# A fused attention and mixture-of-experts kernel: one mask cast moved from VectorE to ScalarE, and the first batch's local queries and keys loaded as runs of nine tokens

## The chip, the cores and the metric

The kernel runs on one core of a Trainium2 chip. The metric is the device time of one execution in microseconds (us), the median of several runs. TensorE (PE) multiplies matrices, VectorE (DVE) and ScalarE (ACT) work element by element and empty PSUM, GpSimd (POOL) does the rest; SyncE (SP) and ACT issue the DMAs that matter here.

## What is computed

Attention over 4 batches, 8 heads, 576 tokens and 64 numbers a head, then a mixture of 8 experts with one expert for each token, then a second MLP over all 2304 tokens. The first four heads see the 32 tokens up to their own (local), the last four see every 32nd token (strided).

```python
scores = scale * np.matmul(q, k.transpose(0, 1, 3, 2))          # (4, 8, 576, 576)
mask_local = (rel >= 0) & (rel < stride)                        # stride = 32
mask_strided = (rel >= 0) & (pos[None, :] % stride == pos[:, None] % stride)
masks = np.stack([mask_local if h < H // 2 else mask_strided for h in range(H)], axis=0)
attn = softmax(np.where(masks, scores, -1e9))
x = (attn @ v).transpose(0, 2, 1, 3).reshape(B * S, H * D)      # 2304 x 512
e_idx = np.argmax(x @ w_gate, axis=1)
out[mask] = gate_w * eom * (relu(x[mask] @ w1[e]) @ w2[e])      # for each expert e
h = np.maximum(out @ w_in, 0.0); result = (h * h) @ w_out
```

## The kernel before

**Stages.** The program runs through attention of batches 0 to 3, then gates and routing, the eight experts, the second MLP, and the stores. Instructions are recorded through a tile framework whose scheduler sets the order on every engine; DMAs that are marked `keep_in_program_order` keep theirs on SP's queue.

**Loads.** `load_s` (L271) brings queries (`qs`) and keys (`ks`) of the strided heads, `load_l` (L283) those of the local heads (`ql`, `kl`), `load_v` the values. For batch 0, `qs` and `ks` are started at L150 and L152 on two queues, and the masks `msk` at L153 on ACT's. A local load is four DMAs per tensor, one a head, each 64 partitions x 9 x 64: partition g gets the tokens g, 64+g, 128+g, ..., nine pieces of 256 bytes.

**Transposes.** `transposes` (L322) makes steps of three: three transposes of 128x128 (L337) into one PSUM tile of the tag `tp` (two buffers), then `evac`, which copies the tile to `qsT`, `ksT`, `qlT` or `klT`, by turns on DVE (L316, L318 where the queries are scaled) and ACT (L320). A `ks` step needs two such copies, for the zero-padded form that the strided scores want. For batch 0 the strided steps come first, the queries' three and then the keys' three, and after each a few products whose result nobody reads (`turn_over`, L229) keep PE occupied. In a local step a 128x128 block holds two heads: the even head in columns 0 to 63, the odd in 64 to 127, so that the transposed block has the even head on partitions 0 to 63 and the odd on 64 to 127.

**Scores.** Each score tile begins with a product of the identity in bf16 and a mask in bf16 (L413 strided, L369 local; both read `cstb`), and the scores are added onto it: L427 for the strided heads (18 columns of the array each, side by side in groups of 32), L382 for the local ones. `cstb` gets the identity at L158 and the two masks at L159, both casts on DVE. After the scores come maximum (L384, L438), exponent (L388, L441, ACT), normalising, transposes of the probabilities (L462, L469) and the products with the values (L486 and L501, 64 columns of the array each). `rw` (L555) is the product for gates.

**At the start of the program** POOL clears padded tiles (L245 to L296) while the first loads arrive.

Of the kernel before, what the change touches and what calls it, by code (L numbers as in the profile page):

```python
# [7 lines left out]
F32 = mybir.dt.float32  # L8
# [4 lines left out]
AF = mybir.ActivationFunctionType  # L13
# [6 lines left out]
B, H, S, HD = 4, 8, 576, 64  # L20
P = 128
# [69 lines left out]
C_ML = C_IO + CAPS[0] - C0  # L91
C_ML0 = C_ML + KW
C_MS = C_ML0 + KW
C_TRI = C_MS + SM
# [3 lines left out]
C_BF = C_ML - P  # L98
# [33 lines left out]
def moe_kernel(ctx, tc, q, k, v, wg, wog, w1, w2, w_in64, w_out64, consts, out, dbg=None):  # L132
    nc = tc.nc
# [5 lines left out]
    fro = front.enter_context(tc.tile_pool(name="att_front", bufs=1, side="right"))  # L139

    cst = const.tile([P, C_ML], F32, name="cst")
    msk = fro.tile([P, C_END - C_ML], F32, name="msk")
# [11 lines left out]
    ident = cst[:, C_ID : C_ID + P]  # L154
    onesb = big.tile([P, P], BF16, name="onesb")
    nc.vector.memset(onesb, 1.0)
    cstb = big.tile([P, C_END - C_BF], BF16, name="cstb")
    nc.vector.tensor_copy(cstb[:, :P], ident)  # L158
    nc.vector.tensor_copy(cstb[:, P : C_TRI - C_BF], msk[:, : C_TRI - C_ML])  # L159
    identb = cstb[:, :P]  # L160
    trib = cstb[:, C_TRI - C_BF : C_IA - C_BF]
    pmh = big.tile([P, LATE, P], BF16, name="pmh")
# [63 lines left out]
    def turn_over(to, n, ins=None):  # L226
        for _ in range(n):
            with tc.issue_after(ins.ins) if ins else nullcontext():
                ins = nc.tensor.matmul(to, onesb, onesb[:, None, :].to_broadcast([P, 4, P]), start=True, stop=True)  # L229
        return ins  # L230
# [21 lines left out]
    NS, NL_ = S * 4 // P, S * 2 // P  # L252
# [6 lines left out]
    for i in range(NPT):  # L259
        if i < 2:  # L260
            x = big.tile([P, 4, 4, NG, SM], F32, name=f"ptp{i}")
            nc.gpsimd.memset(x, 0.0)
            ptp.append(x)
        x = big.tile([P, 4, NG, 32], F32, name=f"prp{i}")
# [3 lines left out]
    def go(o, i, kept=True):  # L268
        ins = nc.sync.dma_start(o, i)
        return tc.keep_in_program_order(ins) if kept else ins  # L270
# [11 lines left out]

    def load_l(b, t):  # L283
        for nm, src in (("q", q), ("k", k)):
            t[nm + "l"] = x = fro.tile([P, NL_, 2, HD], F32, name=f"{nm}l{b}", tag=nm + "l", bufs=1)
            for h in (0, 2, 1, 3):
                to = x[h // 2 * HD : h // 2 * HD + HD, :, h % 2, :]
                go(to, src[b, h].rearrange("(n g) d -> g n d", n=NL_), b < 2)

    def load_v(b, t):  # L290
        t["vs"] = x = vsp[b % 3]
# [12 lines left out]
    def load(b):  # L304
        t = load_s(b)
        load_l(b, t)
        load_v(b, t)
        return t
# [3 lines left out]
    def evac(out_ap, in_ap, scale=None):  # L312
        cnt_ev[0] += 1
        if EVP[cnt_ev[0] % len(EVP)]:
            if scale is None:
                nc.vector.tensor_copy(out_ap, in_ap)  # L316
            else:
                nc.vector.tensor_scalar(out_ap, in_ap, scale, None, op0=ALU.mult)  # L318
        else:
            nc.scalar.activation(out_ap, in_ap, AF.Copy, scale=1.0 if scale is None else scale)  # L320

    def transposes(b, t):  # L322
        t.update(trs[b % 2])
        for kind in "sl":
            steps = [(n0, nm) for n0 in range(0, 9, 3) for nm in "qk"]
            if b == 0:
                steps.sort(key=lambda x: x[1] == "k")
            for n0, nm in steps:
                yield
                ps = pss.tile([P, 3, P], F32, name=f"t{kind}{b}{nm}{n0}", tag="tp")  # L330
                x = t[nm + kind]
                late1 = b == 1 and kind == "s" and n0 == 0
                for i in range(3):
                    n = n0 + i
                    src = x[:, 2 * HD * n : 2 * HD * (n + 1)] if kind == "s" else x[:, n].rearrange("p j d -> p (j d)")
                    with tc.issue_after(lead["pt"].ins) if late1 else nullcontext():
                        ins = nc.tensor.transpose(ps[:, i, :], src, ident)  # L337
                if b == 0 and kind == "s":
                    turn_over(idle, HEAD[1 if (n0, nm) == (6, "q") else 2], ins)
                    lead["ts"] = ins  # L340
                y = t[nm + kind + "T"]
                if kind == "l":
                    y = y.rearrange("d h (n g) -> d n h g", n=9)[:, n0 : n0 + 3]
                    evac(y, ps.rearrange("d n (h g) -> d n h g", h=2), 0.125 if nm == "q" else None)
                    continue
                z = ps.rearrange("d n (h g) -> d h g n", h=4)
                if nm + kind == "ks":
                    y = y.rearrange("d h u (a g n) -> d u a h g n", a=3, n=3)[:, :, n0 // 3]
                    for j in range(2):
                        r = slice(j * HD, (j + 1) * HD)  # L350
                        evac(y[r, j], z[r])
                    continue
                y = y.rearrange("d h (a g n) -> d a h g n", a=3, n=3)[:, n0 // 3]
                evac(y, z, 0.125 if nm == "q" else None)
# [155 lines left out]

    tiles = {0: load_s(0)}
    load_l(0, tiles[0])
    q2, q3 = [], []

# [250 lines left out]
    def route(b, ts, lg, rows):  # L765
# [69 lines left out]
        else:  # L835
            weigh()

    tg = transposes(0, tiles[0])
    for _ in range(2 * 3 + 1):
        next(tg)  # L840
    tiles[1] = load_s(1)
    load_v(0, tiles[0])
    load_l(1, tiles[1])
    tables()
    load_v(1, tiles[1])
    nc.gpsimd.memset(zero, 0.0)
    nc.sync.dma_start(x_d[0].rearrange("(p c) -> p c", c=P), zero)
    for b in range(B):
        t = tiles[b]
        tn = transposes(b + 1, tiles[b + 1]) if b + 1 < B else iter(())  # L850
        for n, ku in enumerate(ORDER[b].split()):
            kind, u = ku[0], int(ku[1:])
# [36 lines left out]
    r = lambda nm, sh, dt=F32: const.tile([P] + sh, dt, name=nm)  # L889
# [370 lines left out]
    def e_l1(k, f):  # L1260
        C = CAPS[k]
        c, i = f * P // UC, f % (UC // P)
        u = ("w1", k, c)
        if k == 0:
            ahead(u, 5, max(units.index(u) + 3 + f % 2, min(units.index(u) + 5, 2 * NF1 // 2)) - units.index(u))
        else:
            with tc.issue_after(lead["relu"].ins), tc.issue_after(lead["step"].ins):
                ahead(u, 5, 3 + f % 2, 7)
        wh, wl = get(("w1", k, c))
        xh, xl = xsp[k]  # L1270
        ps = psm.tile([P, 512], F32, name=f"h{k}_{f}", tag="h", bufs=2)
        for a in range(KD):
            s_ = slice(i * P, (i + 1) * P)
            mm3(ps[:, :C], wh[:, a, s_], wl[:, a, s_], xh[:, a, :C], xl[:, a, :C], a == 0, a == KD - 1)
        hh = raws.tile([P, CAPS[0]], F32R, name=f"hh{k}_{f}", tag="xr", bufs=HB)
        hl = raws.tile([P, CAPS[0]], F32R, name=f"hl{k}_{f}", tag="xr", bufs=HB)
        ia, iv = split_by[units[1 + f]] if k == 0 < f < 4 else (lead["xa"], lead["pm"])
        with tc.issue_after(ia.ins):
            lead["relu"] = nc.scalar.activation(hh[:, :C], ps[:, :C], AF.Relu)  # L1279
        with tc.issue_after(iv.ins):  # L1280
            lead["step"] = nc.vector.scalar_tensor_tensor(  # L1281
                out=hl[:, :C], in0=ps[:, :C], scalar=0.0, in1=hh[:, :C].bitcast(F32), op0=ALU.max, op1=ALU.subtract
            )
        return hh, hl
# [70 lines left out]
    for k in range(E):  # L1355
        for f in range(NF1):
            h = e_l1(k, f)
# [21 lines left out]
            if (k, f) in CONV:  # L1379
                n = CONV.index((k, f))  # L1380
# [335 lines left out]
```

## Time and profile before

| | |
|---|---|
| median of 3 runs | 779.6 us (778.9 to 780.54) |
| the profiled execution | 782.54 us |
| its span, first to last instruction | 780.7 us |
| mean granted TensorE clock | 0.994 of full speed |
| PE busy | 756.5 us, 97% of the span |
| PE's weight loads (PEld) | 678.4 us, 87% |
| DVE, ACT, POOL busy | 565.9, 460.4, 172.8 us |

The profile shows one execution, 2.9 us above the median of the runs. PE's share is high over the whole span, so what matters is where PE has gaps; the views by window and the timeline show those. A row of the timeline gives the start, the length, the engine, the line and operation, output and inputs, and the idle time of the engine before it with what ended it.

### The profile page before, as it was taken

Reading aid. Unit: us, or ns where it says so; the run is one execution under the profiler, and the core shown is the slowest. Engines: PE = TensorE matmul, PEld = TensorE weight load, DVE = VectorE, ACT = ScalarE, POOL = GpSimd, SP = SyncE. Lnnn points to the kernel's source line nnn. Section 1 sums busy time; section 2 is a strip of 40 time slices with the busy share of each in tenths; the row PEclk is TensorE's granted clock in tenths of the full one; section 3 lists DMA queues with packets and bytes.
Section 4 is the critical chain, followed back from the end, with each engine's and each line's share of the span. In section 5 each row is a group of like instructions: output and inputs, shape, how many; then the busy total and the mean of one; then the engine's idle time right before and its main releaser. Section 6 shows DMA issues by size and latency. Waiting matters only on the chain.

```text
span 780.7 us, 14501 instructions
## 1 busy us (share of the span) xinstructions
PE 756.5 (97%) x5429; PEld 678.4 (87%) x5429; DVE 565.9 (72%) x1074; ACT 460.4 (59%) x930; POOL 172.8 (22%) x168
## 2 busy tenths in 40 slices
PE   7999998999999999999999999999999999999995
PEld 4777777899998999999988889888988988989894
DVE  6868787873676888888798989896555687556442
ACT  2745645444553665657687767786555676566443
POOL 6100101036627555320031232122000003000002
PEclk9999999999999999999999999999999999999998
DMA  9999713684988999866454444444322234223002
GB/s 198 169 200 222 134 54 103 220 279 113 224 275 197 302 242 317 282 212 216 129 203 175 149 163 175 144 154 136 127 75 88 82 113 170 75 95 102 0 1 83
DMA packets 104114, 124.86 MB, mean 160 GB/s; under 512 B 39428, under 2 KB 76856, under 8 KB 104040
## 3 DMA queue, kind: packets, MB, share of 16 engines
q1 hardware_dynamic: 95736, 100.42, 45.5%
q0 software_dynamic: 7568, 22.70, 8.6%
q10 hardware_dynamic: 736, 0.76, 0.4%
q8 instruction: 44, 0.72, 0.4%
q14 instruction: 30, 0.25, 0.1%
HBM read 101.82 MB, written 22.04 MB: 159 GB/s over the span
## 4 chain that ended last, share of the span: by engine, by line
PE 56%; issue 30%; DVE 7%; DMA 2%; POOL 2%; ACT 1%; POOLq 0%; SPq 0%; ACTq 0%; DVEq 0%
PE y L1092 5%; PE y L1094 5%; PE y L1093 5%; PE h L1092 5%; PE h L1094 5%; PE h L1093 5%; PE o L1093 2%; PE o L1092 2%; PE o L1094 2%; PE rw L555 2%; POOL out_dram L1436 2%; PE wt L1171 1%; PE sc1l L382 1%; PE lr L732 1%; PE sc2l L382 1%
## 5 line engine op out<-in xcount | busy, mean ns | idle before, releaser
L1092 PE MATMUL o<-hwo,gh 128*128 128x512 f32 x288 | 113.7, 396 | 0.9 <-ACT gh L1406 0.7
L1093 PE MATMUL o<-lwo,gh 128*128 128x512 f32 x288 | 113.5, 395 | 0.0
L1403 ACT ACTIVATE rl<-rl 128x384 f32<-128x384 f32 x96 | 49.6, 517 | 85.7 <-DVE rl L1401 85.7
L1072 DVE TENSOR_TENSOR lw<-rw,hw 128x1024 fp32r<-128x1024 f32 x62 | 83.7, 1352 | 16.4 <-ACT hw L1068 14.6
L1094 PE MATMUL o<-hwo,gl 128*128 128x512 f32 x288 | 84.2, 395 | 0.4 <-DVE gl L1408 0.4
L1092 PE MATMUL h<-xh,hw 128*128 128x416 f32 (+7 forms) x256 | 80.4, 315 | 0.9 <-issue 0.7
L1408 DVE TENSOR_TENSOR gl<-rl,gh 128x384 fp32r<-128x384 f32 x96 | 55.8, 584 | 34.1 <-ACT rl L1407 33.6
L1094 PE MATMUL h<-xh,lw 128*128 128x416 f32 (+7 forms) x256 | 79.4, 310 | 0.4 <-issue 0.4
L1093 PE MATMUL h<-xl,hw 128*128 128x416 f32 (+7 forms) x256 | 79.3, 310 | 0.0
L1436 POOL DMA_INDIRECT out_dram<-ob,idx x18 | 23.1, 1284 | 252.5 <-ACT ob L1435 247.2
L1279 ACT ACTIVATE hh<-h 128x416 fp32r<-128x416 f32 (+7 forms) x64 | 28.2, 441 | 85.8 <-PE h L1094 69.1
L1093 PE MATMUL y<-hl,hw 128*128 128x416 f32 (+7 forms) x256 | 78.6, 310 | 0.0
L1094 PE MATMUL y<-hh,lw 128*128 128x416 f32 (+7 forms) x256 | 78.1, 310 | 0.3 <-issue 0.3
L1092 PE MATMUL y<-hh,hw 128*128 128x416 f32 (+7 forms) x256 | 74.3, 311 | 0.0
L1068 ACT ACTIVATE hw<-rw 128x1024 fp32r<-128x1024 f32 x62 | 65.2, 1055 | 4.4 <-issue 3.8
L1092 PEld LDWEIGHTS o<-hwo,gh 128*128 128x128 f32 x288 | 54.0, 188 | 11.7 <-ACT gh L1406 1.4
L1093 PEld LDWEIGHTS o<-lwo,gh 128*128 128x128 f32 x288 | 54.1, 188 | 10.0 <-DVE lwo L1072 0.5
L1094 PEld LDWEIGHTS o<-hwo,gl 128*128 128x128 f32 x288 | 53.4, 188 | 8.5 <-DVE gl L1408 0.9
L1281 DVE SCALAR_TENSOR_TENSOR hl<-h,hh 128x416 fp32r<-128x416 f32 (+7 forms) x64 | 31.2, 488 | 33.7 <-ACT hh L1279 28.7
L1407 ACT ACTIVATE rl<-rl 128x384 f32<-128x384 f32 x96 | 50.1, 522 | 2.3
L1406 ACT ACTIVATE gh<-rl 128x384 fp32r<-128x384 f32 x96 | 50.0, 521 | 1.9
L1092 PEld LDWEIGHTS h<-xh,hw 128*128 128x128 f32 x256 | 48.1, 188 | 1.2 <-DVE hl L1281 0.5
(626 smaller groups left out, 1926.3 us busy)
## 6 DMA issues: line engine op xcount, KB each, us to landing
rw<-in_moe_w_dram SPq DMA_DIRECT2D x62, 512.0 KB
rwa<-ws_d SPq DMA_DIRECT2D x24, 512.0 KB
rwb<-ws_d SPq DMA_DIRECT2D x24, 384.0 KB
e6wi<-in_moe_w_in_dram SPq DMA_DIRECT2D x32, 256.0 KB
rwo<-wout_d SPq DMA_DIRECT2D x16, 512.0 KB
x_d<-xr SPq DMA_DIRECT2D x18, 256.0 KB
ws_d<-eo POOLq DMA_DIRECT2D x16, 256.0 KB
s0wo<-in_moe_w_out_dram SPq DMA_DIRECT2D x8, 512.0 KB
```

The lines of the kernel that those rows point to most:

```text
L1068: ia = nc.scalar.activation(hi, raw, AF.Copy)
L1072: iv = eng.tensor_tensor(lo, raw, hi.bitcast(F32), op=ALU.subtract)
L1092: kept(nc.tensor.matmul(ps, ah, bh, start=first, stop=False))
L1093: kept(nc.tensor.matmul(ps, ah, bl_, start=False, stop=False))
L1094: lead["sum"] = kept(nc.tensor.matmul(ps, al, bh, start=False, stop=last))
L1279: lead["relu"] = nc.scalar.activation(hh[:, :C], ps[:, :C], AF.Relu)
L1281: lead["step"] = nc.vector.scalar_tensor_tensor(out=hl[:, :C], in0=ps[:, :C], scalar=0.0, in1=hh[:, :C].bitcast(F32), op0=ALU.max, op1=ALU ...
L1403: nc.scalar.activation(rl[:, :HC], src, AF.Relu)
L1406: nc.scalar.activation(hh[:, :HC], rl[:, :HC], AF.Square)
L1407: ia = nc.scalar.activation(rl[:, :HC], rl[:, :HC], AF.Square)
L1408: iv = nc.vector.tensor_tensor(hl[:, :HC], rl[:, :HC], hh[:, :HC].bitcast(F32), op=ALU.subtract)
L1436: ins = nc.gpsimd.indirect_dma_start(out=out[:, :], out_offset=bass.IndirectOffsetOnAxis(ap=idx[:, gt_, 0:1], axis=0), in_=ob, in_offset=None,
```

## The change

**The cast of the masks** leaves DVE. It becomes an ACT instruction that is recorded inside `transposes`, after the three transposes of the first `ks` step.

**The loads of batch 0's local heads** are cut another way. Partition g gets the tokens 9g to 9g+8, one run of 2304 bytes, and the tile is laid out by head, token, number instead of token, head, number. The other batches keep their loads.

**The transposes of these tiles** (batch 0, local) are cut in two. The even head's 64 columns are transposed into partitions 0 to 63 (L340 of the changed kernel), and the odd head's are multiplied with the identity in fp32 into partitions 64 to 127 (L341). So 18 transposes of 128 columns become 18 of 64 columns and 18 products. The copies out of PSUM write tokens 9g+n to their places, in as many instructions as before.

```diff
-    nc.vector.tensor_copy(cstb[:, P : C_TRI - C_BF], msk[:, : C_TRI - C_ML])
+    cstb_masks = lambda: nc.scalar.activation(cstb[:, P : C_TRI - C_BF], msk[:, : C_TRI - C_ML], AF.Copy)
...
     def load_l(b, t):
         for nm, src in (("q", q), ("k", k)):
-            t[nm + "l"] = x = fro.tile([P, NL_, 2, HD], F32, name=f"{nm}l{b}", tag=nm + "l", bufs=1)
+            sh = [P, NL_, 2, HD] if b else [P, 2, NL_, HD]
+            t[nm + "l"] = x = fro.tile(sh, F32, name=f"{nm}l{b}", tag=nm + "l", bufs=1)
             for h in (0, 2, 1, 3):
-                to = x[h // 2 * HD : h // 2 * HD + HD, :, h % 2, :]
-                go(to, src[b, h].rearrange("(n g) d -> g n d", n=NL_), b < 2)
+                r = slice(h // 2 * HD, h // 2 * HD + HD)
+                if b == 0:
+                    go(x[r, h % 2], src[b, h].rearrange("(g n) d -> g n d", n=NL_))
+                else:
+                    go(x[r, :, h % 2, :], src[b, h].rearrange("(n g) d -> g n d", n=NL_), b < 2)
...
                 for i in range(3):
                     n = n0 + i
+                    if kind == "l" and b == 0:
+                        nc.tensor.transpose(ps[:HD, i, :], x[:, 0, n, :], ident)
+                        nc.tensor.matmul(ps[HD:, i, :], x[:, 1, n, :], ident, start=True, stop=True)
+                        continue
...
+                if (b, kind, n0, nm) == (0, "s", 0, "k"):
+                    cstb_masks()
...
                 if kind == "l":
-                    y = y.rearrange("d h (n g) -> d n h g", n=9)[:, n0 : n0 + 3]
-                    evac(y, ps.rearrange("d n (h g) -> d n h g", h=2), 0.125 if nm == "q" else None)
+                    o = "d n h g" if b else "d h g n"
+                    if b:
+                        y = y.rearrange("d h (n g) -> d n h g", n=9)[:, n0 : n0 + 3]
+                    else:
+                        y = y.rearrange("d h (g n) -> d h g n", n=9)[:, :, :, n0 : n0 + 3]
+                    evac(y, ps.rearrange(f"d n (h g) -> {o}", h=2), 0.125 if nm == "q" else None)
                     continue
```

DVE's order at the start, before: the cast stands ahead of the copy of the third query step and of the first copies of the keys.

```order
L318 TENSOR_SCALAR qsT_128<-ts0q_166 128x4x96
L159 CAST cstb<-msk 128x210
L318 TENSOR_SCALAR qsT_128<-ts0q_178 128x4x96
L316 COPY ksT_130<-ts0k_188 64x4x96
L316 COPY ksT_130<-ts0k_195 64x4x96
```

The same piece of DVE's order after the change (lines of the changed kernel, whose numbers are a little higher); the cast is gone.

```order
L322 TENSOR_SCALAR qsT_127<-ts0q_165 128x4x96
L322 TENSOR_SCALAR qsT_127<-ts0q_177 128x4x96
L320 COPY ksT_129<-ts0k_187 64x4x96
L320 COPY ksT_129<-ts0k_195 64x4x96
```

ACT's order after the change: the cast stands between the copy of the second query step and ACT's first copy of the keys. Before, nothing stood there.

```order
L153 DMA msk<-in_consts_dram 128x210
L324 ACT_TABLE_LOAD
L324 ACTIVATE qsT_127<-ts0q_171 128x4x96
L159 ACTIVATE cstb<-msk 128x210
L324 ACTIVATE ksT_129<-ts0k_187 64x4x96
L324 ACTIVATE ksT_129<-ts0k_195 64x4x96
```

PE's order behind the first strided scores, before: `tl0q` and `tl0k` are the PSUM tiles of the local steps of batch 0, `sc0s` the two strided score tiles.

```order
L427 MATMUL sc0s_257<-ksT_130,qsT_128 18x2x18 x32
L337 MATMUL tl0q_302<-cst,ql_156 128x128 x3
L337 MATMUL tl0q_307<-cst,ql_156 128x128 x3
L427 MATMUL sc0s_317<-ksT_130,qsT_128 18x2x18 x27
L337 MATMUL tl0q_312<-cst,ql_156 128x128 x3
L427 MATMUL sc0s_317<-ksT_130,qsT_128 18x2x18 x5
```

The same place after the change, from the last pair of `tl0q_310` to the second score tile and the pairs of `tl0q_318`; the pairs of `tl0q_302`, ahead of them, and the nine of `tl0k` read the same way.

```order
L340 MATMUL tl0q_310<-cst,ql_155 64x128
L341 MATMUL tl0q_310<-cst,ql_155 64x128
L441 MATMUL sc0s_326<-ksT_129,qsT_127 18x2x18 x24
L340 MATMUL tl0q_318<-cst,ql_155 64x128
L341 MATMUL tl0q_318<-cst,ql_155 64x128
L340 MATMUL tl0q_318<-cst,ql_155 64x128
L341 MATMUL tl0q_318<-cst,ql_155 64x128
L340 MATMUL tl0q_318<-cst,ql_155 64x128
L341 MATMUL tl0q_318<-cst,ql_155 64x128
L441 MATMUL sc0s_326<-ksT_129,qsT_127 18x2x18 x8
```

Each transpose of 128 columns has become a transpose and a product by turns. The pairs stand where the steps of three stood, and the groups on PE are otherwise nearly in the same order: 24 and 8 of the second tile's scores instead of 27 and 5.

## Rows read from the trace of the kernel before

**Rows 1.** The page, busy time of an engine, its share of the span, instructions.

```profile
PE 756.5 (97%) x5429; PEld 678.4 (87%) x5429; DVE 565.9 (72%) x1074; ACT 460.4 (59%) x930; POOL 172.8 (22%) x168
```

**Rows 2.** Windows of 10 and 1 us: busy of PE, PEld, DVE, ACT, POOL; clock, DMA, GB/s.

```profile
0.00:10.00 10.00, 8.56 (x37) 3.98 (x37) 4.92 (x6) 2.26 (x3) 9.37 (x12) 1.00 0.94 195
10.00:20.00 10.00, 6.27 (x146) 4.60 (x147) 6.93 (x9) 1.92 (x5) 2.83 (x7) 0.83 1.03 200
20.00:30.00 10.00, 9.56 (x131) 7.39 (x128) 9.04 (x25) 7.73 (x33) 0.96 (x2) 1.00 1.01 182
...
10.00:11.00 1.00, 0.00 (x0) 0.00 (x0) 1.00 (x1) 0.00 (x0) 1.00 (x2) 1.00 1.38 180
...
15.00:16.00 1.00, 0.82 (x3) 0.15 (x1) 0.66 (x2) 0.43 (x1) 0.00 (x0) 0.50 0.81 184
```

**Rows 3.** Timeline of the head of the program, all engines.

```profile
4.68 3.56 POOL L250 MEMSET vsp<- 128x2048 f32 x2
...
6.82 0.56 DVE L318 TENSOR_SCALAR qsT<-ts0q 128x384 f32<-128x384 f32 x1 [2.12 <-PE ts0q L337]
...
8.92 4.04 DVE L159 CAST cstb<-msk 128x210 bf16<-128x210 f32 x1 [1.54 <-DMA msk<-in_consts_dram]
...
9.43 0.48 ACT L320 ACTIVATE ksT<-ts0k 64x384 f32<-64x384 f32 x1 [1.57 <-PE ts0k L337]
...
12.88 0.54 DVE L318 TENSOR_SCALAR qsT<-ts0q 128x384 f32<-128x384 f32 x1
...
13.47 0.55 PE L337 MATMUL ts0k<-cst,ks 128*128 128x128 f32 x3 [3.86 <-DVE qsT L318]
...
16.08 1.35 PE L427 MATMUL sc0s<-ksT,qsT 128*18 128x36 f32 x64 [0.26 <-DVE ksT L316]
```

**Rows 4.** The other cast of masks, L188, at 41.6 us (ns min/median/max).

```profile
L188 DVE CAST cstb<-msk x1: 303/303/303, 41.6 to 41.6; 128x292 bf16<-128x292 f32 x1
```

**Rows 5.** Timeline of PE: the local transposes of batch 0 and their neighbours.

```profile
17.36 0.96 PE L337 MATMUL tl0q<-cst,ql 128*128 128x128 f32 x6
...
18.25 1.20 PE L427 MATMUL sc0s<-ksT,qsT 128*18 128x36 f32 x54
...
20.39 0.82 PE L337 MATMUL tl0k<-cst,kl 128*128 128x128 f32 x6
...
21.54 0.55 PE L337 MATMUL tl0k<-cst,kl 128*128 128x128 f32 x3 [0.32 <-DVE klT L316]
...
22.01 0.78 PE L382 MATMUL sc0l<-klT,qlT 64*64 64x64 f32 x16
```

**Rows 6.** Operations of the tile tl0q: ns min/median/max.

```profile
L337 PE MATMUL tl0q<-cst,ql x9: 272/273/412, 17.4 to 19.7; 128*128 128x128 f32 x9
```

**Rows 7.** Timeline of PE: neighbours of one shape, then of different shapes.

```profile
24.90 0.66 PE L469 MATMUL pt0s<-cst,prp 128*128 128x128 f32 x4
25.39 0.49 PE L337 MATMUL ts1k<-cst,ks 128*128 128x128 f32 x3
...
45.73 0.76 PE L555 MATMUL rw<-igw,xT 128*128 128x144 f32 x4
...
48.86 0.30 PE L427 MATMUL sc1s<-ksT,qsT 128*18 128x36 f32 x2
49.10 0.64 PE L462 MATMUL pt1l<-cst,pr1l 128*96 128x128 f32 x4
49.67 0.30 PE L427 MATMUL sc1s<-ksT,qsT 128*18 128x36 f32 x2
49.90 0.55 PE L337 MATMUL ts2q<-cst,qs 128*128 128x128 f32 x3
```

**Rows 8.** Groups on PE from 40 to 60 us: busy us, mean ns.

```profile
L382 PE MATMUL sc1l<-klT,qlT 64*64 64x96 f32 x56 | 4.6, 254 | 0.0
L555 PE MATMUL rw<-igw,xT 128*128 128x144 f32 x20 | 3.8, 312 | 0.0
```

**Rows 9.** Timeline, SP's queue: the local queries of batch 0.

```profile
3.62 3.58 SPq L269 DMA_DIRECT2D ql<-in_q_dram  x4
```

## The prediction

> **What bounds the kernel now.** I read the page first: PE is busy for 756.5 of 780.7 us [rows 1]. What removes a gap of PE counts, what adds work to PE counts, and what other engines do counts where PE waits for it. The windows show where gaps are [rows 2]: PE is busy for 8.56 us of the first ten, 6.27 of the second and 9.56 of the third. So the second ten microseconds hold the one large hole: from 10 to 11 PE does nothing while DVE and POOL are busy all the time. After the hole the granted clock is at 0.50, the lower of its two levels (1.2 GHz), in the window from 15 to 16.
>
> The timeline names the hole [rows 3]. DVE starts the cast of the masks (L159) at 8.92, when `msk` has landed, and is in it for 4.04 us. Behind it on DVE stands the copy of the last query step, which runs only at 12.88. PE's second key step needs that copy's PSUM buffer and waits 3.86 us for it, until 13.47. The strided scores (L427) then begin at 16.08.
>
> Is it the cast that is slow, or all of DVE? A copy of 128x384 on DVE took 0.56 us at 6.82, in the middle of POOL's memsets, as long as the 0.54 at 12.88. The other cast of masks, 128x292 and thus wider, took 0.30 us at 41.6 [rows 4]. So it is that cast at that place, beside POOL, and the copies are not held with it.
>
> **Part 1, the cast to ACT: a gain at the head.** ACT is idle for 1.57 us until its first copy of the keys at 9.43 [rows 3], and the cast can start when `msk` has landed, 8.92. Its length on ACT for 210 columns is not shown; between the 0.30 us of DVE's 292 columns [rows 4] and the 0.48 us of that copy's 384 I take 0.40. It ends at 9.32, 0.11 before ACT is needed. It costs nothing, and a tenth or two if it is longer.
>
> On DVE the last query copy then no longer waits for 12.88. The key steps follow one another [rows 3]: ACT's copy at 9.43 shows that the first step is done by then, as it stays. The second, 0.55 us, comes behind one idle product, by my estimate at 9.6, so it ends at 10.15 and its copies (0.5 to 0.56) at 10.7. The third needs the buffer of the first, whose two copies, on both engines from 9.43, end at 10.0; so it starts at about 10.3, ends at 10.85, and its copies end at 11.4. The score masks run beside these copies. So L427 starts at 11.6 to 11.9 where it now starts at 16.08: 4.2 to 4.5 us. I allow 3.9 (PE or DVE steps a little worse placed) to 4.8 (the low clock after the hole goes too) and take **4.3 us less**.
>
> **Part 2, pairs in place of transposes: a cost on PE.** Before, the 18 transposes take two steps together and one alone for `tl0q` and the same for `tl0k`. From the start of a group to the start of the next these are 0.89 us (17.36 to 18.25), 0.82 (busy, 20.39) and 0.47 (21.54 to 22.01) [rows 5]; the single step of `tl0q` I count as the last. The sum is 0.89 + 0.47 + 0.82 + 0.47 = 2.65 us.
>
> After, 18 pairs stand there, each a transpose over 64 columns of the array and an fp32 product that fills the other 64. No row shows such a pair, so I bound it. A transpose takes 0.273 us [rows 6] and three of them 0.49 behind others of their shape [rows 7], so they follow each other at (0.49 - 0.273) / 2 = 0.11. The change of shape shows in the neighbours [rows 7]. `pt0s` lasts from 24.90 to 25.56, and `ts1k`, of its shape, starts at 25.39, 0.17 before that end. Between the narrow scores and whole-array transposes the next group starts only 0.06 to 0.07 before the end of the last: 49.16 against 49.10, 49.74 against 49.67, 49.97 against 49.90. So at each change of how the array is divided the pipeline empties almost wholly. The first transpose after it is also longer: three take 0.55 us instead of 0.49.
>
> If each half of a pair is such a change, a pair is:
> - the transpose, 0.27, or 0.33 if the 0.06 that three take longer falls to the first, less the overlap of 0.07: 0.20 to 0.26;
> - the product's two passes (a plain fp32 product shows as two instructions: `sc0s` stands 32 times in the order and 64 in the trace). The first lasts to the start of the second, no less than the 0.11 of a transpose and no more than the (0.76 - 0.31) / 3 = 0.15 of `rw`, four of which last 0.76 us [rows 7] at a mean of 0.31 [rows 8];
> - the second pass, between 0.25 (`sc1l`, 96 columns) and 0.31 (`rw`, 144), less 0.07: 0.18 to 0.24 [rows 8].
>
> That is 0.49 to 0.65 us; I take the middle, 0.57. Eighteen are 8.8 to 11.7, I take 10.2, and less 2.65 this is 6.2 to 9.0, taken **7.5 us more**. It lies on the path: from 20 to 30 us PE has only 0.44 us of gaps [rows 2], of which I let it fill 0.25. The maxima and exponents of batch 0 move back with it, and DVE and ACT have nothing else that could begin earlier instead. The gates, the experts and all that follows wait for attention, and PE is full there [rows 1], so a shift at 28 us arrives at the end.
>
> The Trainium skill, "TensorEngine Tiling (Array Packing)", Key Properties, says that changing the tiling mode drains TensorE. The overlap that falls from 0.17 to 0.07 us agrees with it; by that rule the change is at +3.0, without it at the -0.3 of the second rival below. The same page, Restrictions and Gotchas, says that column tiling excludes transposing fp32 on trn2; no row here shows it, and by it no transpose could run beside a product and the first rival below could not come.
>
> **Part 3, the loads: nothing.** SP issues the four query loads from 3.62 in 3.58 us [rows 9]. Until PE wants `ql`, now at about 12.9, 8 strided and 4 local loads of 144 KB, `msk` and `ident` must have landed, 1.9 MB; at 195 GB/s in the first ten us [rows 2] that is done at 10. The keys, 0.6 MB more at 200 GB/s, are there at 13 and wanted after 17. Runs of 2304 instead of 256 bytes only bring this forward. If their covers were gone they would show as a wait of PE for `ql`; the trace has none at 17.36 [rows 5]. The copies out of PSUM write rows in another order, as the strided steps' copies do now, at the 0.56 and 0.48 us in the rows of the head [rows 3].
>
> **The sum**, against the profiled execution of 782.54 us: -4.3 + 7.5 - 0.25 = +3.0, so 785.5. That execution is 2.9 above the median of the three runs, 779.6; the same difference on the median gives **782.6 us**. Its own range, both ends of both terms not met at once, is +1.4 to +4.8: 781.0 to 784.4.
>
> **The rivals.**
> - *The halves of a pair run side by side*, in two halves of the array, the transpose beside the product. Then a pair is two passes of 0.13, 18 x 0.26 = 4.7, +2.0 net, and the change is -2.3: 777.3, faster. For it: the narrow scores, which lie side by side in the array, follow each other at 1.35 / 64 = 0.02 us [rows 3]. Against: those are all products; a transpose beside a product is nowhere in the trace. It decides if a pair costs less than (2.65 + 4.3) / 18 = 0.39 us. Chance 0.16.
> - *One behind the other without emptying.* Then a pair is 0.11 + 2 x 0.13 = 0.37, 18 are 6.7, +4.0, and the sum -0.3: 779.3, no change that can be told. Against it is the overlap of 0.07 at every change of shape above. Chance 0.12.
> - *The cast is as slow on ACT.* If not DVE beside POOL but the place in time (the loads that arrive, DMA share 1.38 in the window from 10 to 11 [rows 2]) makes it 4 us, ACT's copy of the keys is held as DVE's was, nothing is gained, and it is +7.3: 786.9. Against: ACT's copy at 9.43 took 0.48 in that same time [rows 3]. Chance 0.04.
>
> **The numbers.** A measurement of this kernel can tell about 0.2%, 1.56 us, from no change. The forecast has 0.62, of which about 0.08 lies within 0.2%; the side-by-side case has 0.16, a third of it within 0.2%; the one-behind-the-other case, 0.12, is nearly all within; the slow cast, 0.04, is slower; 0.06 is for what I don't see, most of it faster. Faster 0.11 + 0.04 = 0.15, same 0.08 + 0.05 + 0.11 = 0.24, slower the other 0.61. The range takes the forecast's own and the first two rivals down to 777.0: 777.0 to 784.4. As the cases have both signs, the forecast's own 781.0 to 784.4 is the one to hold it to.
>
> **What would show it.** Right: the wait of 3.86 us is gone, L159 is an ACT row of about 0.4 us, L427 starts between 11.6 and 11.9 at the full clock (2.4 GHz), the 18 transposes and 36 passes of `tl0q` and `tl0k` take some 10 us from group to group, and the first local scores, at 22.01 now, start at about 25. Wrong: pairs that start under 0.39 us apart, an ACT copy of the keys later than 9.6, PE waiting for `ql` or `kl`, or a clock at 0.50 in a stretch where it is now full.

## The result: slower by 5 us, by more than forecast

The changed kernel takes 785.33 us in the median of 4 runs (784.86 to 786.14), the kernel before 779.98 (778.9 to 780.54): a ratio of 1.0068, with an interval of 1.0055 to 1.008, or +5.35 us. The way was forecast, the size was not: +3.0, with a range that ended at 784.4.

The page of the changed kernel has PE busy 8.4 us longer than before [rows 1] in a span that is 3.6 us longer.

```profile
span 784.3 us, 14572 instructions
...
PE 764.9 (98%) x5465; PEld 682.5 (87%) x5465; DVE 559.2 (71%) x1073; ACT 460.2 (59%) x931; POOL 172.4 (22%) x168
```

In windows of 10 us of the changed kernel (the columns of [rows 2]) the hole is gone. PE is busy for 8.89 us of the second ten instead of 6.27 [rows 2], the clock is granted in full there, and from 20 us on PE is full, with fewer instructions in it: 93 in the third ten instead of 131.

```profile
10.00:20.00 10.00, 8.89 (x150) 5.57 (x147) 3.70 (x8) 2.64 (x6) 2.82 (x7) 1.00 0.86 222
20.00:30.00 10.00, 9.83 (x93) 5.84 (x93) 3.99 (x11) 2.64 (x6) 0.67 (x1) 1.00 0.96 158
```

The timeline of the changed kernel shows the parts. The strided queries are transposed from 7.68 on, the cast is on ScalarE and takes 0.38 us, the strided scores (L441) start at 13.66 instead of 16.08 [rows 3], and the pairs follow each other at 15.52 - 14.92 = 0.60 and 16.11 - 15.52 = 0.59 us. The first local scores start at 28.56 instead of 22.01 [rows 5], and batch 1's local queries (`tl1q`) at 38.73.

```profile
7.68 0.49 PE L345 MATMUL ts0q<-cst,qs 128*128 128x128 f32 x3
...
9.95 0.38 ACT L159 ACTIVATE cstb<-msk 128x210 bf16<-128x210 f32 x1 [0.71 <-DMA msk<-in_consts_dram]
...
13.66 1.33 PE L441 MATMUL sc0s<-ksT,qsT 128*18 128x36 f32 x64 [0.70 <-DVE ksT L320]
...
14.92 0.30 PE L340 MATMUL tl0q<-cst,ql 128*64 128x128 f32 x1
...
15.15 0.43 PE L341 MATMUL tl0q<-cst,ql 128*64 128x128 f32 x2
...
15.52 0.30 PE L340 MATMUL tl0q<-cst,ql 128*64 128x128 f32 x1
...
16.11 0.30 PE L340 MATMUL tl0q<-cst,ql 128*64 128x128 f32 x1
...
28.56 1.44 PE L396 MATMUL sc0l<-klT,qlT 64*64 64x64 f32 x32 [0.17 <-DVE klT L320]
...
38.73 0.55 PE L345 MATMUL tl1q<-cst,ql 128*128 128x128 f32 x3
```

The delay settles early: `tl1q` starts 5.73 us later than in this execution of the kernel before (33.00, shown below), and the first expert's products (`h`) 5.37 us later. The first of these in the kernel before:

```profile
148.62 0.46 PE L1092 MATMUL h<-xh,hw 128*128 128x416 f32 x1
```

and in the changed kernel:

```profile
153.99 0.46 PE L1106 MATMUL h<-xh,hw 128*128 128x416 f32 x1
```

That the span differs by 3.6 only comes for the most part from the execution of the kernel before that was profiled first. It lost 0.31 + 1.09 = 1.40 us of PE time later on, from 235 to 265 us, which the same stretch of the changed kernel, 5 us later, did not. These are windows of 15 us, with columns as before, of the kernel before:

```profile
235.00:250.00 15.00, 14.69 (x99) 14.51 (x98) 10.53 (x17) 6.85 (x11) 9.89 (x10) 1.00 0.87 216
250.00:265.00 15.00, 13.91 (x90) 13.36 (x89) 10.46 (x18) 9.81 (x18) 9.37 (x12) 1.00 0.93 238
```

and of the changed kernel:

```profile
240.00:255.00 15.00, 15.00 (x102) 14.97 (x101) 11.86 (x19) 8.25 (x13) 9.85 (x11) 1.00 0.88 222
255.00:270.00 15.00, 15.00 (x101) 15.00 (x100) 8.92 (x16) 8.99 (x16) 8.58 (x11) 1.00 0.91 218
```

### The profile page after: what moved, and what is told of

Same layout as the page of the kernel before. It is cut to its first block, busy times and chain, and to the rows that moved or that the text cites. A ratio compares the mean times of both kernels' runs of the same rounds, so it can differ in the third digit from the quotient of the medians.

```text
span 784.3 us, 14572 instructions
## 1 busy us (share of the span) xinstructions
PE 764.9 (98%) x5465; PEld 682.5 (87%) x5465; DVE 559.2 (71%) x1073; ACT 460.2 (59%) x931; POOL 172.4 (22%) x168
## 4 chain that ended last, share of the span: by engine, by line
PE 58%; issue 30%; DVE 7%; POOL 2%; DMA 1%; ACT 1%; POOLq 0%; SPq 0%; DVEq 0%
PE y L1106 5%; PE h L1106 5%; PE y L1108 5%; PE y L1107 5%; PE h L1108 5%; PE h L1107 5%; PE o L1107 2%; PE o L1106 2%; PE o L1108 2%; PE rw L569 2%; POOL out_dram L1450 2%; PE idle L229 1%; PE wt L1185 1%; DVE xl L1325 1%; PE sc1l L396 1%
## 5 line engine op out<-in xcount | busy, mean ns | idle before, releaser
L1086 DVE TENSOR_TENSOR lw<-rw,hw 128x1024 fp32r<-128x1024 f32 x62 | 82.1, 1327 | 16.6 <-ACT hw L1082 16.5
```

Of the source, the lines that this page charges most:

```text
L1086: iv = eng.tensor_tensor(lo, raw, hi.bitcast(F32), op=ALU.subtract)
```

## The experiments

Ratios below are to runs of the kernel before on the same chip, whose medians were 781.2 us (`cast_only`, `pairs_pieces`, `grouped`, `two_products`), 780.53 (`cast_vl_late`, `runs_pairs_dve`, `dve_max`, `after_again`) and 781.34 (`half_runs`).

### The cast alone, and the old loads with the rest

`cast_only` has the cast on ScalarE and nothing else of the change.

```diff
-    nc.vector.tensor_copy(cstb[:, P : C_TRI - C_BF], msk[:, : C_TRI - C_ML])
+    cstb_masks = lambda: nc.scalar.activation(cstb[:, P : C_TRI - C_BF], msk[:, : C_TRI - C_ML], AF.Copy)
...
+                if (b, kind, n0, nm) == (0, "s", 0, "k"):
+                    cstb_masks()
```

> The kernel before with only the cast of the masks on ScalarE; loads and transposes as before. My theory: the hole of PE behind the cast goes and nothing is added, so the first strided scores start between 11.7 and 13.7 us instead of 16.08, and the time is 2.4 to 4.4 us under the kernel before (775.6 to 777.6). Rival 1 (the late first transposes of the changed kernel, 7.68 instead of 6.27, come from the new loads, which take DMA time from the strided queries): here they start at 6.3 and the scores at about 12.2. Rival 2 (they come from the clock of TensorE, which rose at 7.0 instead of 3.97 in that execution and made the 17 idle products longer): the start follows the time at which the idle products get short, whatever the loads are. Rival 3 (the gain is given back later in attention): the scores start early and the time is that of the kernel before.

Measured: 781.56 us, ratio 0.9993 (0.9982 to 1.0005). Rival 3 has it. In its profile the scores start at 12.48 instead of 16.08, and PE stays 3.75 us ahead of the kernel before until 29 us. Then it stands still for 2.95 us, for the local queries of batch 1, and the clock is granted at 0.66 over the ten microseconds that hold most of this wait. The products behind it are longer: 16 of `o0s` take 1.23 us here, and 0.72 in the kernel before (33.86, shown below). So the first expert's products come at 149.95, 1.33 us later than in the first profile of the kernel before, though `tl1q` came 0.63 us earlier. The timeline of PE in this run:

```profile
12.48 1.30 PE L429 MATMUL sc0s<-ksT,qsT 128*18 128x36 f32 x64 [0.71 <-DVE ksT L316]
...
29.12 0.30 PE L415 MATMUL sc1s<-cstb 128*128 128x288 bf16 x1
32.37 0.87 PE L337 MATMUL tl1q<-cst,ql 128*128 128x128 f32 x3 [2.95 <-DMA ql<-in_q_dram]
...
34.02 1.23 PE L503 MATMUL o0s<-ptp,vsp 128*64 128x72 f32 x16
```

and its windows:

```profile
20.00:30.00 10.00, 9.30 (x130) 7.28 (x126) 9.27 (x26) 9.81 (x44) 1.65 (x2) 1.00 1.02 182
30.00:40.00 10.00, 7.63 (x103) 6.25 (x103) 2.86 (x8) 2.73 (x8) 0.51 (x1) 0.66 0.93 166
```

`pairs_pieces` has all of the change but the nine-token runs.

```diff
-                r = slice(h // 2 * HD, h // 2 * HD + HD)
-                if b == 0:
-                    go(x[r, h % 2], src[b, h].rearrange("(g n) d -> g n d", n=NL_))
-                else:
-                    go(x[r, :, h % 2, :], src[b, h].rearrange("(n g) d -> g n d", n=NL_), b < 2)
+                to = x[h // 2 * HD : h // 2 * HD + HD, :, h % 2, :]
+                go(to, src[b, h].rearrange("(n g) d -> g n d", n=NL_), b < 2)
...
-                        nc.tensor.transpose(ps[:HD, i, :], x[:, 0, n, :], ident)
-                        nc.tensor.matmul(ps[HD:, i, :], x[:, 1, n, :], ident, start=True, stop=True)
+                        nc.tensor.transpose(ps[:HD, i, :], x[:, n, 0, :], ident)
+                        nc.tensor.matmul(ps[HD:, i, :], x[:, n, 1, :], ident, start=True, stop=True)
...
```

> The changed kernel with the old loads of 256-byte pieces: pairs and the cast on ScalarE stay, only the nine-token runs go. My theory: the loads are hidden, so the time is that of the changed kernel within 0.7 us (784.6 to 786.0), and a pair takes 0.59 us as there. Rival 1 (the runs delay the strided queries): 1.4 us under the changed kernel, 783.9, and the first transposes start at 6.3. A third view (the pieces are too slow for the earlier start of the local transposes): PE waits for ql or kl and the time is above the changed kernel.

Measured: 787.64 us, ratio 1.0064 (1.0048 to 1.008), the changed kernel's 1.0068 within the interval. (In us it is above the 786.0 expected, but on this chip the kernel before is 1.2 us slower too.) So beside the pairs the runs are worth nothing that can be told, and they do not delay the start either: the first transposes begin at 6.73 here, at 6.04 in a second profile of the changed kernel and at 7.68 in the first.

### What a pair costs

`grouped` puts the three transposes of a step first and its three products behind them.

```diff
                     if kind == "l" and b == 0:
                         nc.tensor.transpose(ps[:HD, i, :], x[:, 0, n, :], ident)
-                        nc.tensor.matmul(ps[HD:, i, :], x[:, 1, n, :], ident, start=True, stop=True)
                         continue
...
+                if kind == "l" and b == 0:
+                    for i in range(3):
+                        nc.tensor.matmul(ps[HD:, i, :], x[:, 1, n0 + i, :], ident, start=True, stop=True)
```

> The changed kernel with the three transposes of a step first and its three products after them, so that a step divides the array anew twice instead of six times. My theory (each change of the division waits until the instruction before is done): a step takes 0.165 + 0.109 + 0.23 + 0.16 + 4 x 0.107 + 0.203 = 1.30 us instead of 1.78, six steps 2.9 us less, 782.4. Rival (the product itself costs what the pair costs more, the change of division nothing): 1.78 us a step and 785.3.

Measured: 783.6 us, ratio 1.0025 (1.0012 to 1.0038), 0.0043 under the changed kernel's, which is 3.4 us (2.7 against the 1.0059 of the changed kernel's second set of runs, below). The same 9 passes of a step now take 15.37 - 14.12 = 1.25 us, where three pairs took 1.78. PE's timeline of this run, two groups of one step and the start of the next:

```profile
14.12 0.52 PE L340 MATMUL tl0q<-cst,ql 128*64 128x128 f32 x3
14.57 0.87 PE L347 MATMUL tl0q<-cst,ql 128*64 128x128 f32 x6
15.37 0.52 PE L340 MATMUL tl0q<-cst,ql 128*64 128x128 f32 x3
```

`two_products` makes the even head a product as well.

```diff
-                        nc.tensor.transpose(ps[:HD, i, :], x[:, 0, n, :], ident)
+                        nc.tensor.matmul(ps[:HD, i, :], x[:, 0, n, :], ident, start=True, stop=True)
```

> The changed kernel with a product by the identity in place of each 64-column transpose too, so that both halves are products, in two halves of the array, and nothing in a step divides the array anew. It has 72 passes where the changed kernel has 54 instructions. My theory: passes in the two halves run beside one another, a pass every 0.055 to 0.11 us, so a step of 12 takes 0.9 to 1.5 us instead of 1.78 and the time is 780.0 to 783.7. Rival (the passes of the products are what costs, not the change of division): 18 more passes of 0.11 to 0.16 us, 2 to 3 us above the changed kernel, 787.3 to 788.3.

Measured: 781.39 us, ratio 0.9996 (0.9983 to 1.001): 5.6 us under the changed kernel (4.9 against 1.0059), with 18 passes more. The two halves start 0.01 us apart, and six pairs of products take 15.44 - 13.98 = 1.46 us, 0.24 each with the exit, against 0.59. So a good part of a pair's price was the dividing anew: with two changes a step a pair is 1.25 / 3 = 0.42 us. The 0.24 has two causes, which this run does not separate: nothing inside a step divides anew, and the two halves run side by side. An estimate separates them. The six product passes of a step of `grouped` follow each other at (0.87 - 0.27) / 5 = 0.12 us, so three passes without a change would take 0.36; of the 0.59, then, 0.23 is the two changes, and what is below 0.36 comes from running side by side. PE's timeline of this run, the first four passes, the last, and what follows:

```profile
13.98 0.32 PE L340 MATMUL tl0q<-cst,ql 128*64 128x128 f32 x1
13.99 0.32 PE L341 MATMUL tl0q<-cst,ql 128*64 128x128 f32 x1
14.14 0.27 PE L340 MATMUL tl0q<-cst,ql 128*64 128x128 f32 x1
14.15 0.27 PE L341 MATMUL tl0q<-cst,ql 128*64 128x128 f32 x1
...
15.24 0.27 PE L341 MATMUL tl0q<-cst,ql 128*64 128x128 f32 x1
15.44 0.77 PE L441 MATMUL sc0s<-ksT,qsT 128*18 128x36 f32 x26
```

### What bounds the head

`cast_vl_late` is the cast alone with the local values of batch 0 loaded later.

```diff
-    load_v(0, tiles[0])
+    load_v(0, tiles[0], "s")
     load_l(1, tiles[1])
+    load_v(0, tiles[0], "l")
...
```

> The kernel with only the cast on ScalarE, and the local values of batch 0 loaded behind the local queries and keys of batch 1 instead of ahead of them. In the run of the cast alone PE was 3.75 us early until 29 us and then waited 2.95 us for the local queries of batch 1, in a stretch in which the DMA engines were busy all the time. Theory (the gain of the head is given back to the loads of batch 1): with these loads ahead of the values that wait goes, the gain stays, and the time is 2 to 4 us under the kernel before. Rival (the DMA engines as a whole are late, not one load): PE waits for the values at the first products with them (o0l, 35.1 us in the kernel before) instead, and the time is again that of the kernel before.

Measured: 781.13 us, ratio 1.0008 (0.999 to 1.0026). The rival has it: `tl1q` starts at 29.27 without a wait, and then the products with the values wait four times for `vl`, and the clock falls as well. But the profile is of the longest of twelve executions: 785.08 us, at a mean granted clock of 0.991. The shortest took 778.89 at 0.998, and no profile shows how long it waited. So that these waits give the whole gain back is shown for one execution and, for the others, only by the median. The waits of PE in this run from 20 to 60 us (in total, times, longest):

```profile
PE o0l L491 <- DMA vl<-in_v_dram: 2.3, 4, 0.8
```

and its windows:

```profile
30.00:40.00 10.00, 7.58 (x93) 5.42 (x92) 2.80 (x7) 2.65 (x7) 0.51 (x1) 0.77 0.95 174
40.00:50.00 10.00, 10.00 (x137) 7.16 (x137) 5.25 (x17) 3.89 (x14) 0.00 (x0) 0.72 1.10 203
```

`runs_pairs_dve` is the changed kernel with the cast back on VectorE, and `dve_max` the kernel before with the cast written as a maximum.

```diff
-    cstb_masks = lambda: nc.scalar.activation(cstb[:, P : C_TRI - C_BF], msk[:, : C_TRI - C_ML], AF.Copy)
+    nc.vector.tensor_copy(cstb[:, P : C_TRI - C_BF], msk[:, : C_TRI - C_ML])
...
```

```diff
-    nc.vector.tensor_copy(cstb[:, P : C_TRI - C_BF], msk[:, : C_TRI - C_ML])
+    nc.vector.tensor_tensor(cstb[:, P : C_TRI - C_BF], msk[:, : C_TRI - C_ML], msk[:, : C_TRI - C_ML], op=ALU.max)
```

> The changed kernel with the cast of the masks back on VectorE; runs and pairs stay. Theory: the cast lasts until POOL is done (about 12.9 us) whatever else is changed, the strided scores start at about 16.1, 2.4 to 3.9 us later than in the changed kernel, and PE is full from there on, so it is 2.4 to 3.9 us slower than the changed kernel: 1.010 to 1.012 of the kernel before. Rival (with the pairs, PE is held up by them so long that the head does not matter): the ratio of the changed kernel, 1.007.

> The kernel before with the cast of the masks on VectorE written as the maximum of the masks with themselves, an operation of two inputs, in place of a copy. Theory (it is this form of copy, from SBUF to a narrower type, that cannot run while POOL works; the copies out of PSUM are not held): the operation takes under 1 us at about 9, the strided scores start at 12 to 12.5, and then the wait for the loads of batch 1 comes as in the run of the cast alone, so the time is that of the kernel before within 0.2%. Rival (VectorE is held there whatever it does with SBUF while POOL works): it takes about 4 us again and the scores start at 16.1.

Measured: 786.16 us, ratio 1.0063 (1.0041 to 1.0085) for the first, and 781.48 us, 1.0003 (0.9989 to 1.0018), for the second. The theory on the first falls: the cast on VectorE took 0.47 us in that profile, beside the same memsets on POOL, and the scores started at 13.51. The rival's ratio came, but not its case: the head was short in this execution, so it does not show that a long head would not matter. In the second the maximum took 0.38 us and PE then waited 3.5 us for the local queries of batch 1, as expected of the theory. But since the copy can be short too, that does not show that its form matters. The timeline of the first run:

```profile
8.89 0.47 DVE L159 CAST cstb<-msk 128x210 bf16<-128x210 f32 x1 [0.28 <-DMA msk<-in_consts_dram]
...
13.51 1.29 PE L439 MATMUL sc0s<-ksT,qsT 128*18 128x36 f32 x64 [0.70 <-DVE ksT L320]
```

and the cast of the second (ns min/median/max):

```profile
L159 DVE TENSOR_TENSOR cstb<-msk x1: 379/379/379, 9.1 to 9.1; 128x210 bf16<-128x210 f32 x1
```

So there are three further profiles of the kernel before. The changed kernel was profiled a second time too (`after_again`).

> The kernel before, a further profile. Theory (the cast of 4.04 us is chance: in the run with the cast back on VectorE it took 0.47 us beside the same memsets): in some of three such profiles the cast takes under 1 us, and PE then waits about 3 us for the local queries of batch 1 at 29 to 33 us instead. Rival (it is always 4 us in this kernel): 4 us in all three, and no such wait.

> The kernel before, a second further profile; each theory expects of it what it expects of the first: under 1 us and a later wait in some of the three, or 4 us in all of them.

> The kernel before, a third further profile; each theory expects of it what it expects of the first: under 1 us and a later wait in some of the three, or 4 us in all of them.

> The changed kernel once more, for a second profile beside runs of the kernel before on the same chip. If the late start of its first transposes (7.68) was the clock of TensorE in that one execution, they start at 6.3 to 7.7 here, at the end of the idle products, and those get short at another time than 7.0; if it comes from the new loads, they start at 7.7 again. Ratio 1.0055 to 1.008 as before.

In two of the three profiles of the kernel before the cast takes 0.72 and 0.40 us and there is no hole at 10 us. PE waits 3.51 and 2.37 us for the local queries of batch 1 instead. In the third it takes 3.82 us, and ends at 12.95 like the 12.96 of the first profile [rows 3]. In all four, `tl1q` starts between 32.79 and 34.34. PE's timeline of the first profile of the kernel before:

```profile
33.00 0.49 PE L337 MATMUL tl1q<-cst,ql 128*128 128x128 f32 x3
...
33.86 0.72 PE L501 MATMUL o0s<-ptp,vsp 128*64 128x72 f32 x16
```

VectorE's cast and PE's row in the first further profile:

```profile
9.11 0.72 DVE L159 CAST cstb<-msk 128x210 bf16<-128x210 f32 x1 [0.91 <-DMA msk<-in_consts_dram]
...
33.53 0.87 PE L337 MATMUL tl1q<-cst,ql 128*128 128x128 f32 x3 [3.51 <-DMA ql<-in_q_dram]
```

in the second:

```profile
9.13 3.82 DVE L159 CAST cstb<-msk 128x210 bf16<-128x210 f32 x1 [1.20 <-DMA msk<-in_consts_dram]
...
34.34 0.52 PE L337 MATMUL tl1q<-cst,ql 128*128 128x128 f32 x3 [0.23 <-DMA ql<-in_q_dram]
```

and in the third:

```profile
9.43 0.40 DVE L159 CAST cstb<-msk 128x210 bf16<-128x210 f32 x1 [0.83 <-DMA msk<-in_consts_dram]
...
32.79 0.52 PE L337 MATMUL tl1q<-cst,ql 128*128 128x128 f32 x3 [2.37 <-DMA ql<-in_q_dram]
```

The changed kernel's second run gave 785.67 us and a ratio of 1.0059 (1.0041 to 1.0077). Its scores started at 12.87 and `tl1q` at 37.94. ACT's cast waited for the masks until 9.75 in this execution, and ACT's first copy of the keys stood behind it:

```profile
9.75 0.38 ACT L159 ACTIVATE cstb<-msk 128x210 bf16<-128x210 f32 x1 [2.15 <-DMA msk<-in_consts_dram]
10.04 0.84 ACT L324 ACTIVATE ksT<-ts0k 64x384 f32<-64x384 f32 x2
...
11.15 0.55 PE L345 MATMUL ts0k<-cst,ks 128*128 128x128 f32 x3 [1.26 <-DVE ksT L320]
```

### A version that is a little faster than both

`half_runs` has the cast on ScalarE, runs for the keys alone, and two products in place of their transposes.

```diff
-            sh = [P, NL_, 2, HD] if b else [P, 2, NL_, HD]
+            sh = [P, 2, NL_, HD] if b == 0 and nm == "k" else [P, NL_, 2, HD]
...
-                if b == 0:
+                if b == 0 and nm == "k":
                     go(x[r, h % 2], src[b, h].rearrange("(g n) d -> g n d", n=NL_))
...
-                    if kind == "l" and b == 0:
-                        nc.tensor.transpose(ps[:HD, i, :], x[:, 0, n, :], ident)
+                    if kind == "l" and b == 0 and nm == "k":
+                        nc.tensor.matmul(ps[:HD, i, :], x[:, 0, n, :], ident, start=True, stop=True)
                         nc.tensor.matmul(ps[HD:, i, :], x[:, 1, n, :], ident, start=True, stop=True)
...
```

> The cast on ScalarE, nine-token runs for the local keys of batch 0 alone, and for them two products in place of each transpose; the local queries keep their 256-byte pieces and whole transposes. Theory (the time of the first 35 us is bounded by PE's own work and by the loads in front of batch 1's local queries, whichever is later): half the products cost about 0.95 us on PE instead of 1.9, half the small pieces are gone (2304 packets of 30 ns on 16 engines, 4.3 us), which is more than the 2.95 us that PE waited in the run of the cast alone, so there is no such wait, and the time is 2 to 3 us under the kernel before. Rival (the loads are late all the same): PE waits for ql of batch 1 for 1 us or more and the time is that of the kernel before.

Measured: 780.36 us against 781.34, ratio 0.9985 (0.9976 to 0.9994), so about 1 us less, the only version whose whole interval lies under the kernel before. The expected 2 to 3 was too much: `tl1q` starts at 32.16 here, only 0.6 to 2.2 us before the 32.79 to 34.34 of the four profiles of the kernel before. In its windows PE has no gap from 20 to 40 us, and it waits for no load there.

```profile
20.00:30.00 10.00, 10.00 (x161) 8.18 (x157) 8.58 (x23) 7.80 (x34) 0.89 (x2) 1.00 0.98 167
30.00:40.00 10.00, 10.00 (x141) 7.52 (x137) 5.49 (x17) 5.83 (x21) 1.27 (x2) 1.00 0.94 178
```

## Why the forecast was right in its way and wrong in its size

**Part 2, the pairs: right.** I took 0.57 us a pair from a range of 0.49 to 0.65; it is 0.59. Eighteen are 3.56 + 1.78 + 3.52 + 1.78 = 10.64 us from group to group, +8.0 instead of +7.5. That each half waits for the other to end was the mechanism: a transpose of 0.30 us lets the product start after 0.23, the overlap of 0.07 that I read from other neighbours. The Trainium skill, "TensorEngine Tiling (Array Packing)", Key Properties, says that changing the tiling mode drains TensorE; the 1.25 us of a grouped step against 1.78 agrees with it. The first and the second rival, side by side and one behind the other without emptying, did not come. A product beside a product does run that way, at 0.24 us a pair.

**Part 1, the step that failed: "take 4.3 us less".** The strided scores started 2.42 us earlier in one profile of the changed kernel and 3.21 in the other, so the term was 1.9 and 1.1 us too large. That is most of the miss: -2.42 + 8.0 - 0.25 = +5.3, and with 3.21 it is +4.5, where the median gave +5.35 and `tl1q` is 5.73 and 4.94 late. Three things were wrong in the term.

The first is the start. I let PE's first transposes stay where they were. They stand behind the 17 idle products, and these took 6.79 us in the changed kernel's profile and 5.25 before. They start 0.43 us apart at first and 0.22 later, and the step from one to the other came at 3.97 us in the first profile of the kernel before and about 7 in that of the changed kernel. It was 3.9 in the second profile of the changed kernel, and about 6.7 in the third further profile of the kernel before, so it is not the change. As long as the hole ended with POOL's memsets, that moment did not matter; without the hole it reaches the scores. The first transposes start at 7.68 instead of 6.27 in the first profile of the changed kernel, 1.41 us late, and at 6.04 in the second, 0.23 early. That the one execution which I read had them early was luck. The idle products in the timeline of the kernel before:

```profile
1.05 5.25 PE L229 MATMUL idle<-onesb 128*128 128x512 bf16 x17 [1.05 <-DVE onesb L156]
```

and of the changed kernel:

```profile
1.05 6.79 PE L229 MATMUL idle<-onesb 128*128 128x512 bf16 x17 [1.05 <-DVE onesb L156]
```

The second is the way from the first transposes to the scores. My times give 5.3 to 5.6 us for it (6.27 to 11.6 and 11.9). It took 13.66 - 7.68 = 5.98 in the first profile, and 5.98 to 6.01 in every other without the hole except `after_again`. There it took 6.83, and that is the third thing: I let the masks land at 8.92 and wrote that the cast on ACT costs nothing, but ACT waited for them until 9.75, and its copy of the keys started at 10.04, some 0.9 us after PE had finished the step (8.65 + 0.49 = 9.14).

**A second mistake of the same step does not show in this number.** It is what stands behind the hole. I wrote that a shift at 28 us arrives at the end, since PE is full there. In that profile PE waited for no load because the hole let the loads come in. The DMA engines were busy without a pause (DMA share 1.01 to 1.03 from 10 to 30 us [rows 2]), and with PE 3.75 us ahead the local queries of batch 1 are late: that is the run of the cast alone. Where I costed the hole's end I should have asked what is late next, and priced it: the start of `tl1q` in the kernel before is 33.00 and 34.34 us with the hole, 33.53 and 32.79 without it. So the gain does not add up with whatever else is done. `tl1q` starts at the later of two times: when the loads are there, 32.4 to 34.3, and when PE's own work is done, which the pairs bring to 37.9 to 38.7. The cast on ScalarE alone takes PE's way to 29.3 (`cast_vl_late`, where nothing waits before it), which the loads swallow, and behind the wait the clock is low. In the changed kernel PE's work is the later by far and PE waits for no load, so there the sum of a gain and a cost holds and only its sizes were wrong.

**Part 3, the loads: right for what it says.** No transpose waited for batch 0's `ql` or `kl`. That the loads behind them could be late I did not see. With all of the small pieces as runs, or half of them, SP issues the local queries of batch 1 at 21.71 and 22.99 (`two_products`, `half_runs`), against 25.01 in the run of the cast alone, and PE does not wait for them. But PE's own work is longer there too, so that it wants them at 32.2 and not at 29.4, and in the run of the cast alone they were there at 32.37. No run has the two products with the old pieces, so what the runs are worth is not shown; the pairs as they are written cost more than it.

**The third rival**, a cast that is as slow on ScalarE, did not come: 0.38 us, against the 0.40 taken.

**What stays open.** Why the copy on VectorE is held until POOL is done in some executions and not in others: it started at 8.92 and 9.13 where it was held, at 8.89, 9.11 and 9.43 where it was not. Nor is the +5.35 us accounted for to the last microsecond. It lies between the 4.9 and 5.7 by which `tl1q` is late in the two profiles of the changed kernel, but that is against the first profile of the kernel before. Against all four `tl1q` is 3.6 to 5.9 us late and the first expert's products are 2.9 to 5.4 (153.22 and 153.99, against 148.62 to 150.34). The profiled executions of the kernel before, 782.05 to 783.07 us, are all longer than its medians, so none of them shows how an execution near the median runs.

## What to carry to other kernels

A stall in one profiled execution is a price only if it is in the others too and if nothing stands right behind it; look at several executions, and ask which transfer arrives just in time because of the stall. A full share of the DMA engines is a bound that no wait shows as long as another one covers it. Two instructions that divide TensorE's array differently should not alternate (0.59 us a pair here): make both of one kind (0.24), or group them (0.42).

## What the runs showed that I had not expected

- A copy from SBUF on VectorE beside the same memsets on POOL takes 0.40 to 0.72 us or 3.82 to 4.04 us, from execution to execution. When long, it ended at 12.95 and 12.96, after POOL's last instruction of that stretch. When short, it too ended 0.12 to 0.13 us after the end of a POOL memset (at 9.83, 9.83 and 9.36), and the next memset was 0.12 us longer than elsewhere: the cast seems to get in where one POOL instruction ends and the next begins, at the first such place, or the second, or not until the last. That is read from five profiles and was not tested; the maximum of `dve_max` ended at 9.46, at no such place. POOL in the first profile of the kernel before:

```profile
9.64 1.07 POOL L262 MEMSET ptp<- 128x1152 f32 x1
...
12.23 0.60 POOL L166 COPY igw<-cst 128x512 f32<-128x512 f32 x1
```

and in the first further profile, where the cast ended at 9.83:

```profile
9.64 1.19 POOL L262 MEMSET ptp<- 128x1152 f32 x1
```

- In the run of the cast alone PE's wait of 2.95 us cost more than its length, for the products behind it ran slower, with the clock granted at 0.66.
- Two fp32 products by the identity, in two halves of the array, cost 0.24 us where a transpose and a product cost 0.59, though they have one pass more.
- The idle products at the start of the program get short at 3.9 to about 7 us, from execution to execution, while the column of the granted clock stands at 1.00.
